# An attention and Fourier mix on one core: stack DMAs in SP's queue, and later steps for a unit's output

## The chip, the cores and the metric

The kernel runs on one core of one Trainium2 chip. The metric is the device time of one execution in microseconds (us); the kernel before has three runs, and their median is the figure. TensorE does the matrix products, VectorE (DVE), ScalarE (ACT) and GpSimd (POOL) the elementwise work, and SyncE (SP) issues most DMAs.

## What is computed

The input `A_x` has 2048 rows of 640. The output mixes two branches with a gate per row; the inputs are in float32. Cut to what matters:

```python
x = A_x
g = sigmoid((x * gate_w).sum(-1, keepdims=True))
q, k, v = split_heads(x @ wqkv)                # 32 heads of 20
p = softmax(q @ k.T * 20 ** -0.5)              # 2048 x 2048 for each head
a = merge_heads(p @ v) @ wo
re, im = x @ hid_re.T, x @ hid_im.T            # DFT along the 640
b = seq_re @ re - seq_im @ im                  # DFT along the 2048, real part
return g * a + (1 - g) * b
```

## The kernel before

**Stages.** A head stage makes queries and keys (`qk_tile`), values (`v_pair`) and the first ten tiles of the hidden DFT, and stores them in scratch memory (`qk_scr`, `v_scr`, `a_scr`). Then comes one long loop over the attention, in which the rest of the Fourier branch is done as filling work, and at last a tail: the product with `wo` and the gate. Values that need more than one pass are split in two float32r parts (`split`).

**Units and steps.** The attention is done in 32 units. A unit `n` is a pair of heads (`p = n // 2`) with one half of the queries (1024). It has 32 steps: 16 blocks of 128 keys by two chunks of 512 queries. A step multiplies scores of both heads (line 685, two matmuls), and ScalarE exponentiates them from PSUM (line 687). The row maxima that the exponential needs are found 41 steps (`LEAD`) ahead of it: the scores are made a first time the other way round (line 159), and VectorE reduces them (line 161). When all maxima of a unit are there, `max_chain` transposes them, splits them in `m1` and `m2`, and two steps later four small DMAs write them as extra rows into the query stack (lines 201 and 202). The scores of line 685 read these rows, so that the maximum is subtracted inside the product.

**Cycles.** Four steps make a cycle, in the order that the string `ORDER` gives: `e` is a score for the exponential, `m` one for the maximum, `F` a place for filling matmuls (hidden DFT, line 301, in the first 54 cycles; from cycle 57 the sequence DFT, line 523), and `B` a burst: the product of `p` and `v` for two key blocks (`av_step`, line 448), reading out finished DFT tiles, and the maxima's chain. Five PSUM banks go round among all scores.

**Places of everything else.** `at_step(i, fn)` puts `fn` into the program where step `i` begins. It sets no time: each engine works through its own instructions in the order written, and waits only for what an instruction needs. An engine can so be ahead of the steps or behind them, and what stands behind a waiting instruction on SP or GpSimd waits too.

**The stacks.** The two heads of a pair lie in one tile of keys (`kst`) and one of queries (`qst`), 128 partitions by 2048, with two buffers of each. `load_stack(p)` yields the twelve DMAs that fill them for pair `p`: four for the keys (two of 320 KB, two planes of 20 rows to 40 partitions, and two of 160 KB, 20 rows), four for the first half of the queries, and four for the second half (160 and 80 KB each). `begin` spreads them over the steps of the pair before, every other step from 2 to 24, on GpSimd's queue (line 643). The maxima of the new pair begin at step 64 - 41 = 23 of that pair; by then the first eight must be there.

**The end of a unit.** `unit_end` (line 453) copies the sums out of PSUM into `o` (line 455) and puts seven operations at steps after it: store the row sums (`store_l`), load them back spread over 128 partitions (`load_l`), their reciprocal on VectorE (`recip`), store that (`store_r`), load it back repeated (`load_r`, four DMAs), multiply on GpSimd (`norm`), store the result (`store_o`, four DMAs). All DMAs are on SP's queue, for the last unit on GpSimd's. `o`, `lc` and `rb` have one buffer each.

**The sequence DFT.** It is done in 56 blocks (`UNITS`) of 16 filling steps (`dft_step`); a block lasts about 14 steps of the attention. At `s == 0` it loads the output tiles that it will be added to (`yt`, line 511, four buffers); every eight filling steps it loads the DFT's coefficients (`load_c`, line 413), which GpSimd adds up and splits half a block later (lines 419, 102, 103). The block's result `m` is read out of PSUM in a burst; `finish_y` adds it on GpSimd (line 554) five steps later and puts the store of the tile four steps behind that (line 558). `load_a` (line 428) brings the hidden DFT's results for the next product. The raw tiles of these loads (`raw`, three buffers) are shared with the read-out of the hidden DFT (line 309).

Of the kernel before, what the change touches and what calls it, by code (L numbers as in the profile page):

```python
# [10 lines left out]
F32 = mybir.dt.float32  # L11
R = mybir.dt.float32r
# [6 lines left out]
P = 128  # L19
# [7 lines left out]
HE = D // 2  # L27
VW = 2 * (DH + 1)
KROWS = 3 * DH
NU = 2 * NP  # L30
# [25 lines left out]
UNITS = len(PRODUCTS) * HT  # L56


def f32(ap):
    return ap.bitcast(F32)  # L60
# [3 lines left out]
def mix_kernel(ctx: ExitStack, tc: tile.TileContext, xa, wqk, wb, cdft, wo, out):  # L64
    nc = tc.nc
    pe, act, dve, pool, sp = nc.tensor, nc.scalar, nc.vector, nc.gpsimd, nc.sync
    ctx.enter_context(tc.manual_schedule())

    def pools(**kw):
        return ctx.enter_context(tc.tile_pool(**kw))  # L70

    const = pools(name="const", bufs=1)
    small = pools(name="small", bufs=1)
# [9 lines left out]
    y_scr = dram.tile([NS, P, D], F32, name="y_scr")  # L83
# [28 lines left out]
    def bank():  # L112
        return ps_w.tile([P, 512], F32, name=f"ps{next(turn) % 5}")
# [13 lines left out]
    def load_stack(p):  # L127
        kt, qt = kst[p % 2], qst[p % 2]
        u = S // 2
        for t, o, two, one, cs in ((kt, D, 0, 2, slice(0, S)), (qt, 0, 1, 0, slice(0, u)), (qt, 0, 1, 0, slice(u, S))):  # L130
            for h in range(2):
                r = (2 * p + h) * DH
                b = 64 * h
                rows = slice(o + r, o + r + DH)
                yield f32(t[b + two * DH : b + (two + 2) * DH, cs]), qk_scr[:, rows, cs]
                yield f32(t[b + one * DH : b + (one + 1) * DH, cs]), qk_scr[0, rows, cs]

    def q_unit(n):
        u = n % 2 * (S // 2)
        return qst[n // 2 % 2][:, u : u + S // 2]  # L140

    mx, nms, ends = {}, {}, []
    now, later = [-1], {}

    def at_step(i, fn):
        later.setdefault(i, []).append(fn)
# [43 lines left out]
    def max_chain(n):  # L190
        q = q_unit(n)
        pt = bank()[:16, :P]
        pe.transpose(pt, nms.pop(n), ident)
        m1 = small.tile([16, P], R, name="m1", bufs=2)
        m2 = small.tile([16, P], R, name="m2", bufs=2)
        split(m1, m2, pt, dve, dve)

        def rows():
            for h in range(2):
                b = 64 * h + KROWS  # L200
                sp.dma_start(f32(q[b : b + 1, :]), f32(m1[8 * h : 8 * h + 8, :]))
                sp.dma_start(f32(q[b + 1 : b + 2, :]), f32(m2[8 * h : 8 * h + 8, :]))

        if now[0] < 0:
            rows()
        else:
            at_step(now[0] + 2, rows)


    pa = pools(name="att", bufs=1)  # L210
# [193 lines left out]
    cfin, rest = [], []  # L404

    def load_c(g):
        n, j = divmod(g, 2)
        n, t = divmod(n, HT)
        raws = []
        for i, (_, th, ri) in enumerate(PRODUCTS[n][0]):  # L410
            raw = apool[0].tile([P, 1024], F32, name="raw2", bufs=2) if i and apool else raw_tile()
            o = (2 * ri + j) * 1024
            sp.dma_start(raw, cdft[th * HT + t, :, o : o + 1024])
            raws.append(raw)

        def finish():
            c = cparts[g] = part_tile()
            if len(raws) > 1:
                pool.tensor_tensor(raws[0], raws[0], raws[1], op=ALU.add if PRODUCTS[n][0][1][0] > 0 else ALU.subtract)  # L419
            split(c[:, 0], c[:, 1], raws[0], pool, pool)  # L420

        return finish
# [28 lines left out]
            unit_end(i, n)  # L451

    def unit_end(i, n):
        o = pa.tile([P, 512], F32, name="o")
        act.activation(o, av, AF.Copy)
        lc = pa.tile([P, 16], F32, name="lc")
        rb = pa.tile([P, 512], F32, name="rb")

        q = pool if n == NU - 1 else sp

        def store_l():
            q.dma_start(l_scr[n], o.rearrange("(j r) c -> j r c", j=4)[:, DH])

        def load_l():
            q.dma_start(lc, l_scr[n].rearrange("j (a b) -> (j a) b", b=16))

        def recip():
            dve.reciprocal(lc, lc)

        def store_r():  # L470
            q.dma_start(r_scr[n].rearrange("j (a b) -> (j a) b", b=16), lc)

        def load_r():
            for j in range(4):
                q.dma_start(rb[32 * j : 32 * j + 32, :], r_scr[n, j : j + 1].to_broadcast([32, 512]))

        def norm():
            pool.tensor_tensor(o, o, rb, op=ALU.mult)  # L478

        def store_o():  # L480
            for qc in range(2):
                for h in range(2):
                    j = 2 * qc + h
                    t0 = (n % 2) * (S // 2) + qc * 512
                    r = (2 * (n // 2) + h) * DH
                    q.dma_start(o_scr[r : r + DH, t0 : t0 + 512], o[32 * j : 32 * j + DH, :])

        steps = (1, 4, 10, 12, 15, 23, 25) if n < NU - 2 else (1, 4, 10, 12, 15, 19, 21)
        for k, fn in zip(steps, (store_l, load_l, recip, store_r, load_r, norm, store_o)):
            if n == NU - 1:  # L490
                rest.append(fn)
            else:
                at_step(i + k, fn)
# [7 lines left out]
    def dft_step(g):  # L501
        n, t, s = g // NS // HT, g // NS % HT, g % NS
        if s == 0:
            new_y(0), new_y(1)
            outs[n, t] = []
            for _, th, hf in PRODUCTS[n][2]:
                tt = th * HT + t
                y = None
                if (tt, hf) in signs:
                    y = apool[0].tile([P, HE], F32, name="yt", bufs=4)  # L510
                    sp.dma_start(y, y_scr[tt, :, hf * HE : (hf + 1) * HE])
                outs[n, t].append(y)
        if s % 8 == 0 and g // 8 + 3 < 2 * UNITS:
            cfin.append(load_c(g // 8 + 3))
        if s % 8 == 4 and cfin and g // 8 + 2 < 2 * UNITS:
            cfin.pop(0)()
        c = cparts[g // 8]
        cs = slice((s % 8) * P, (s % 8 + 1) * P)
        a = at[n % 2, s]
        for z, (cz, az) in enumerate(((0, 0), (0, 1), (1, 0))):  # L520
            for h in range(2):
                r = slice(64 * h, 64 * h + 64)
                pe.matmul(yp[h][:, :HE], c[r, cz, cs], a[r, az], start=s == 0 and z == 0, stop=s == NS - 1 and z == 2)  # L523
            if z < 2:
                yield
        w = g % (HT * NS) - 16
        if n + 1 == len(PRODUCTS) and w >= 0:
            d, r = divmod(w, 8)
            if r == 0 and d < ND:
                wos[d] = raw_tile()[:, :D]  # L530
                sp.dma_start(wos[d], wo[:, d])
            if r == 5 and d < ND:
                raw = wos.pop(d)
                for h in range(2):
                    wos[d, h] = a_tile(1, 2 * d + h)
                    split(wos[d, h][:, 0], wos[d, h][:, 1], raw[:, h * HE : (h + 1) * HE], pool, pool)
        if s == NS - 1:
            m = apool[0].tile([P, HE], F32, name="m", bufs=2)
            y0, y1 = yp[0][:, :HE], yp[1][:, :HE]

            def read():
                act.activation(m, y0, AF.Copy)
                dve.tensor_tensor(m, y1, m, op=ALU.add)  # L543

            extras.append((now[0], read))
            for out_, y in zip(PRODUCTS[n][2], outs.pop((n, t))):
                extras.append((now[0] + 5, functools.partial(finish_y, out_, t, m, y)))
        yield

    def finish_y(target, t, m, y):  # L550
        sg, th, hf = target
        tt = th * HT + t
        if (tt, hf) in signs:
            pool.tensor_tensor(y, y, m, op=ALU.add if sg == signs[tt, hf] else ALU.subtract)  # L554
        else:
            signs[tt, hf] = sg
            y = m
        at_step(now[0] + 4, functools.partial(sp.dma_start, y_scr[tt, :, hf * HE : (hf + 1) * HE], y))

    preps = []  # L560

# [69 lines left out]
    def begin(i):  # L631
        now[0] = i
        n, s = divmod(i, 32)
        for fn in later.pop(i, ()):
            fn()
        if s % 2 == 0:
            flush()
        if s == 0 and n % 2 == 0:
            p = n // 2
            if p + 1 < NP:  # L640
                at_step(i + 6, functools.partial(load_v, p + 1))
                for j, args in enumerate(load_stack(p + 1)):
                    at_step(i + 2 + 2 * j, functools.partial(pool.dma_start, *args))
        if i < total:
            pts[n, s // 2, s % 2] = pair_tile()

# [90 lines left out]
    for tt in range(NS):  # L737
        y, o = ys.pop(tt), ops.pop(tt)
# [53 lines left out]
```

## Time and profile before

| what | value |
|---|---|
| median of three runs | 1954.19 us (1954.18 to 1955.42) |
| the profiled execution's own time | 1953.52 us |
| its span, first to last instruction | 1951.7 us |
| TensorE's granted clock, mean | 0.997 of full speed |
| HBM read and written | 213.81 and 63.70 MB |
| SP waiting in line 635 for `DVE raw L310` (pacing by the read-out) | 236.3 us, 52 times |
| SP waiting in line 471 for the reciprocal (pacing) | 149.5 us, 28 times |
| SP waiting in line 475 for the stored reciprocals to land | 52.0 us, 18 times |
| GpSimd waiting in line 478 for `rb` | 73.7 us, 6 times |

The span is what the profile covers; the run's own time has some 1.8 us around it. A row of the timeline is: start in us, length, engine, line of the kernel, operation, output<-inputs, shapes, count, and in brackets the idle time before it and what ended that. A row of the waits is: engine and line, what it waited for, us in total, times, the longest. A row of the windows is: from:to, length, then busy time and count for PE, PEld (weight loads), DVE, ACT and POOL, then the granted clock, the busy share of the 16 DMA engines and GB/s. A wait of SP or of GpSimd is no loss by itself: most of these waits only keep them from running further ahead.

### The profile page before, as it was taken

How to read it: one execution, taken by the hardware profiler on the slowest of the kernel's cores; microseconds unless marked ns; L12 is line 12 of the kernel's file. 1: busy time of each engine (PE TensorE's matmuls, PEld its weight loads, DVE VectorE, ACT ScalarE, POOL GpSimd, SP SyncE). 2: the span in 40 equal slices, each digit the busy share in tenths (PEclk: the TensorE clock that was granted, in tenths of full speed). 3: DMA queues.
4: the chain of work that ended last, by engine and by line, in shares of the span. 5: the costliest groups of instructions: out<-in, count | busy, mean ns of one | idle time of the engine just before them, and what ended most of it. 6: DMA issues, size and time to landing. Idle time of an engine off the chain costs nothing. (4 is left out here: it accounts for less than half of the span.)

```text
span 1951.7 us, 43695 instructions
## 1 busy us (share of the span) xinstructions
PE 1918.5 (98%) x17080; PEld 1375.4 (70%) x17080; DVE 1454.1 (75%) x2419; ACT 1211.8 (62%) x2337; POOL 1045.8 (54%) x975
## 2 busy tenths in 40 slices
PE   8999999999999999999999999999999999999999
PEld 7987767777775667666666666666666666666679
DVE  4144568889887888888888878888888887888323
ACT  4221147777776676666776766676766776776741
POOL 1210001111005989457469968995786789787512
PEclk9999999999999999999999999999999999999999
DMA  7763321212114584435356746664554565454355
GB/s 224 173 172 127 130 100 46 78 61 74 47 58 141 170 228 152 122 116 149 97 173 199 196 154 189 212 177 123 149 171 125 183 169 181 154 149 147 98 165 179
DMA packets 196414, 281.02 MB, mean 144 GB/s; under 512 B 73272, under 2 KB 137816, under 8 KB 194288
## 3 DMA queue, kind: packets, MB, share of 16 engines
q1 hardware_dynamic: 158992, 246.20, 40.8%
q0 software_dynamic: 37216, 32.03, 6.7%
q8 instruction: 134, 2.20, 0.5%
q14 instruction: 72, 0.59, 0.1%
HBM read 213.81 MB, written 63.70 MB: 142 GB/s over the span
## 5 line engine op out<-in xcount | busy, mean ns | idle before, releaser
L161 DVE TENSOR_REDUCE mx<-ps 128x1 f32<-128x512 f32 x2048 | 1287.4, 683 | 197.4 <-PE ps L159 178.8
L687 ACT ACTIVATE p<-ps 128x512 f32<-128x512 f32 x2048 | 1080.9, 598 | 443.4 <-PE ps L159 241.2
L159 PE MATMUL ps<-kst,qst 60*128 60x512 f32 x2048 | 776.1, 427 | 8.0 <-DVE mx L161 3.2
L685 PE MATMUL ps<-qst,kst 62*128 62x512 f32 x2048 | 700.7, 422 | 5.8 <-DMA qst<-m 4.2
L523 PE MATMUL yp<-a,part 64*128 64x320 f32 x5376 | 687.6, 309 | 0.1
L523 PEld LDWEIGHTS yp<-a,part 64*128 64x128 f32 x5376 | 593.7, 186 | 15.3 <-DVE m L543 0.3
L448 PE MATMUL av<-p,v 128*21 128x512 f32 x4096 | 494.4, 599 | 0.1
L685 PEld LDWEIGHTS ps<-qst,kst 62*128 62x128 f32 x2048 | 335.5, 185 | 215.2 <-DVE mx L161 181.9
L159 PEld LDWEIGHTS ps<-kst,qst 60*128 60x128 f32 x2048 | 364.5, 185 | 38.2 <-DVE mx L161 11.8
L103 POOL TENSOR_TENSOR part<-raw,part 128x1024 fp32r<-128x1024 f32 x112 | 267.2, 2386 | 9.0
L448 PEld LDWEIGHTS av<-p,v 128*21 128x21 f32 x4096 | 98.3, 100 | 226.8 <-issue 223.1
L301 PE MATMUL yp<-wb,xs 64*128 64x320 f32 x1920 | 237.4, 309 | 3.7 <-ACT raw L309 3.5
L301 PEld LDWEIGHTS yp<-wb,xs 64*128 64x128 f32 x1920 | 206.8, 187 | 8.9 <-ACT raw L309 4.1
L419 POOL TENSOR_TENSOR raw<-raw,raw 128x1024 f32<-128x1024 f32 x78 | 187.4, 2402 | 17.3 <-DMA raw<-in_cdft 11.8
L102 POOL CAST part<-raw 128x1024 fp32r<-128x1024 f32 x112 | 116.4, 1039 | 116.8 <-PE yp L523 87.4
L102 POOL CAST wb<-raw 128x966 fp32r<-128x966 f32 (+1 forms) x4 | 3.4, 856 | 215.8 <-PE ps L159 215.8
L554 POOL TENSOR_TENSOR yt<-yt,m 128x320 f32<-128x320 f32 x64 | 55.5, 878 | 111.3 <-DVE m L543 104.2
L478 POOL TENSOR_TENSOR o<-o,rb 128x512 f32<-128x512 f32 x32 | 41.4, 1294 | 134.5 <-DMA rb<-r_scr 73.7
L103 POOL TENSOR_TENSOR a<-araw,a 128x320 fp32r<-128x320 f32 x112 | 97.8, 873 | 9.0
L103 DVE TENSOR_TENSOR p<-ps,p 128x512 fp32r<-128x512 f32 x40 | 27.5, 691 | 94.1 <-ACT p L100 91.4
L106 PE MATMUL ps<-xs,part 128*128 128x512 f32 x200 | 80.2, 401 | 7.8 <-ACT xs L100 6.1
L100 ACT ACTIVATE p<-ps 128x512 fp32r<-128x512 f32 x40 | 23.7, 597 | 101.4 <-PE ps L108 101.4
(67 smaller groups left out, 1331.8 us busy)
## 6 DMA issues: line engine op xcount, KB each, us to landing
raw<-in_cdft SPq DMA_DIRECT2D x192, 512.0 KB
araw<-a_scr SPq DMA_DIRECT2D x192, 160.0 KB
qk_scr<-p SPq DMA_DIRECT2D x40, 512.0 KB
kst<-qk_scr POOLq DMA_DIRECT2D x32, 320.0 KB, 12.3
qst<-qk_scr POOLq DMA_DIRECT2D x64, 160.0 KB, 8.2
a_scr<-raw SPq DMA_DIRECT2D x64, 160.0 KB
yt<-y_scr SPq DMA_DIRECT2D x64, 160.0 KB
y_scr<-yt SPq DMA_DIRECT2D x64, 160.0 KB
```

The source lines that it names most:

```text
L102: e1.tensor_copy(dst1, src)
L103: e2.tensor_tensor(dst2, src, f32(dst1), op=ALU.subtract)
L106: pe.matmul(ps, st1, mv1, start=first, stop=False)
L159: pe.matmul(ps, q[b : b + KROWS, qt * P : (qt + 1) * P], k[b : b + KROWS, kc * 512 : (kc + 1) * 512], start=True, stop=True)
L161: return lambda: dve.tensor_reduce(mx[n][:, h, qt, kc : kc + 1], ps, axis=AX.X, op=ALU.max)
L301: pe.matmul(yp[h][:, :HE], xs[r, xz, d, cs], w[r, wz, d, :HE], start=d == 0 and z == 0, stop=d == ND - 1 and z == 2)
L419: pool.tensor_tensor(raws[0], raws[0], raws[1], op=ALU.add if PRODUCTS[n][0][1][0] > 0 else ALU.subtract)
L448: pe.matmul(av[32 * j : 32 * j + DH + 1, :], v[:, kt, h * (DH + 1) : (h + 1) * (DH + 1)], pp[qc][:, h, :], start=kt == 0, stop=kt == NS - 1)
L523: pe.matmul(yp[h][:, :HE], c[r, cz, cs], a[r, az], start=s == 0 and z == 0, stop=s == NS - 1 and z == 2)
L554: pool.tensor_tensor(y, y, m, op=ALU.add if sg == signs[tt, hf] else ALU.subtract)
L685: pe.matmul(pt, k[b : b + KROWS + 2, kt * P : (kt + 1) * P], q[b : b + KROWS + 2, qc * 512 : (qc + 1) * 512], start=True, stop=True)
L687: act.activation(pts[n, kt, qc][:, h], pt, AF.Exp, scale=float(DH) ** -0.5)
```

## The change

The twelve stack DMAs of a pair go from GpSimd's queue to SP's, at steps 4, 6, 8, 10 to 14 (the first eight) and 34, 37, 40 and 43 (the last four). A unit's seven operations go from steps 1, 4, 10, 12, 15, 23, 25 to 6, 10, 16, 23, 27, 34, 45, except for the last two units, and `o` gets a second buffer. `m1` and `m2` get one buffer in place of two. The load of `yt` goes from the first to the ninth filling step of a block, and behind the coefficient loads of the first. The store of a finished tile goes from four to eight steps behind its update.

```diff
@@ -191,8 +191,8 @@
-        m1 = small.tile([16, P], R, name="m1", bufs=2)
-        m2 = small.tile([16, P], R, name="m2", bufs=2)
+        m1 = small.tile([16, P], R, name="m1")
+        m2 = small.tile([16, P], R, name="m2")
@@ -451,7 +451,7 @@
     def unit_end(i, n):
-        o = pa.tile([P, 512], F32, name="o")
+        o = pa.tile([P, 512], F32, name="o", bufs=2)
@@ -485,7 +485,7 @@
-        steps = (1, 4, 10, 12, 15, 23, 25) if n < NU - 2 else (1, 4, 10, 12, 15, 19, 21)
+        steps = (6, 10, 16, 23, 27, 34, 45) if n < NU - 2 else (1, 4, 10, 12, 15, 19, 21)
         for k, fn in zip(steps, (store_l, load_l, recip, store_r, load_r, norm, store_o)):
@@ -503,6 +503,11 @@
         if s == 0:
             new_y(0), new_y(1)
             outs[n, t] = []
+        if s % 8 == 0 and g // 8 + 3 < 2 * UNITS:
+            cfin.append(load_c(g // 8 + 3))
+        if s % 8 == 4 and cfin and g // 8 + 2 < 2 * UNITS:
+            cfin.pop(0)()
+        if s == 8:
             for _, th, hf in PRODUCTS[n][2]:
@@ -510,10 +515,6 @@
                     sp.dma_start(y, y_scr[tt, :, hf * HE : (hf + 1) * HE])
                 outs[n, t].append(y)
-        if s % 8 == 0 and g // 8 + 3 < 2 * UNITS:
-            cfin.append(load_c(g // 8 + 3))
-        if s % 8 == 4 and cfin and g // 8 + 2 < 2 * UNITS:
-            cfin.pop(0)()
@@ -555,7 +556,7 @@
-        at_step(now[0] + 4, functools.partial(sp.dma_start, y_scr[tt, :, hf * HE : (hf + 1) * HE], y))
+        at_step(now[0] + 8, functools.partial(sp.dma_start, y_scr[tt, :, hf * HE : (hf + 1) * HE], y))
@@ -639,8 +640,8 @@
                 at_step(i + 6, functools.partial(load_v, p + 1))
-                for j, args in enumerate(load_stack(p + 1)):
-                    at_step(i + 2 + 2 * j, functools.partial(pool.dma_start, *args))
+                for j, args in zip((4, 6, 8, 10, 11, 12, 13, 14, 34, 37, 40, 43), load_stack(p + 1)):
+                    at_step(i + j, functools.partial(sp.dma_start, *args))
```

## The prediction

> **What bounds the kernel now.** I read the page first: span, busy shares, DMA queues.
>
> ```profile
> span 1951.7 us, 43695 instructions
> ## 1 busy us (share of the span) xinstructions
> PE 1918.5 (98%) x17080; PEld 1375.4 (70%) x17080; DVE 1454.1 (75%) x2419; ACT 1211.8 (62%) x2337; POOL 1045.8 (54%) x975
> ...
> q1 hardware_dynamic: 158992, 246.20, 40.8%
> ```
>
> TensorE is marked busy in 98% of the span, so at most 33 us lie open as idle, and the change adds and removes no matmul, reduce or exponential. What it can win or lose is waits of TensorE. The view of its waits says on whom:
>
> ```profile
> PE ps L685 <- DMA qst<-m: 4.2, 2, 3.3
> PE yp L301 <- ACT raw L309: 3.5, 2, 2.7
> PE ps L159 <- DVE mx L161: 3.2, 4, 1.2
> PE ps L106 <- ACT v L280: 3.0, 2, 2.6
> PE ps L159 <- DMA qst<-qk_scr: 2.4, 1, 2.4
> ```
>
> Line 685 waited for the rows of maxima, line 159 for a query stack: both are transfers that this change moves. The lines 106 are the head of the kernel, which it doesn't touch. A wait costs more than its idle time, so I measure by units: from one copy of `av` (line 455) to the next is one unit of 32 steps. The timeline of ScalarE:
>
> ```profile
> 526.02 0.60 ACT L455 ACTIVATE o<-av 128x512 f32<-128x512 f32 x1 [0.58 <-issue]
> 576.25 0.60 ACT L455 ACTIVATE o<-av 128x512 f32<-128x512 f32 x1 [0.59 <-issue]
> 631.47 0.60 ACT L455 ACTIVATE o<-av 128x512 f32<-128x512 f32 x1 [0.95 <-POOL a L102]
> ...
> 1033.45 0.60 ACT L455 ACTIVATE o<-av 128x512 f32<-128x512 f32 x1 [0.51 <-issue]
> 1083.21 0.60 ACT L455 ACTIVATE o<-av 128x512 f32<-128x512 f32 x1 [0.91 <-POOL raw L419]
> 1137.88 0.60 ACT L455 ACTIVATE o<-av 128x512 f32<-128x512 f32 x1 [2.07 <-POOL part L102]
> ...
> 1585.82 0.60 ACT L455 ACTIVATE o<-av 128x512 f32<-128x512 f32 x1 [0.91 <-issue]
> 1640.62 0.60 ACT L455 ACTIVATE o<-av 128x512 f32<-128x512 f32 x1 [0.81 <-POOL part L103]
> ```
>
> A clean unit takes 576.25 - 526.02 = 50.23 us with hidden-DFT fills and 1083.21 - 1033.45 = 49.76 us with sequence-DFT fills, 1.555 us a step. Three units are long: 55.22, 54.67 and 54.80 us, so 4.99, 4.91 and 5.04 too much. All three begin where a pair begins, that is, where a stack is loaded. In the second the wait was 3.3 us; the rest is the clock, in the table of windows:
>
> ```profile
> 1133.60:1137.00 3.40, 3.07 (x14) 0.93 (x18) 0.00 (x0) 1.09 (x2) 3.34 (x3) 0.50 0.13 45
> ```
>
> After the wait TensorE got a clock of 0.50 for 3.4 us and lost 1.7 us: 3.3 + 1.7 = 5.0, the 4.91. A wait for a DMA here costs its length plus up to 1.7 us.
>
> **Part 1: output steps and y stores.** Why were the rows late at 1134? GpSimd's and SP's timelines:
>
> ```profile
> 1123.34 1.30 POOL L478 TENSOR_TENSOR o<-o,rb 128x512 f32<-128x512 f32 x1
> ...
> 1124.67 1.42 SPq L486 DMA_DIRECT2D o_scr<-o  x4
> ...
> 1127.83 0.68 SPq L201 DMA_DIRECT2D qst<-m  x1
> ```
>
> The normalisation stands at step +23 of its unit, the store of `o` at +25, the rows at +26. GpSimd reached the normalisation 1123.34 - 1083.21 = 40.1 us after the copy; SP stood at the store until then, and the rows left at +44.6 us. Over the run SP stood there often:
>
> ```profile
> SPq L486 <- POOL o L478: 108.0, 25, 14.9
> ```
>
> After the change the normalisation stands at +34 and the store at +45, thirteen steps into the next unit. Ahead of the rows stands the store of reciprocals (+23), whose input is made at +16, seven steps (10.9 us) earlier; the load of `rb` (+27) comes behind them. The y stores go from +4 to +8, so they too leave 6.2 us more for a late GpSimd. I take the 4.91 us as gone. The four row DMAs then go out near step 26, six steps or 9.3 us before the unit that reads them, and the next thing late would be a row DMA slower than that. What the later store needs: `o` must live past +32, hence its second buffer; without it ScalarE's copy would wait 45 - 32 = 13 steps, 20 us a unit. `m1` and `m2` with one buffer are rewritten a unit (50 us) after the row DMAs that read them. Both cost nothing. The y load moves to the middle of a block, about 7 + 5 = 12 steps (18.7 us) ahead of its reader on GpSimd, with GpSimd 54% busy as cover: nothing.
>
> The reciprocal moves from +10 to +16 on VectorE:
>
> ```profile
> L468 DVE RECIPROCAL lc<-lc 128x16 f32<-128x16 f32 x32 | 7.8, 243 | 10.3 <-DMA lc<-l_scr 10.3
> ```
>
> ```profile
> 897.94 0.25 DVE L468 RECIPROCAL lc<-lc 128x16 f32<-128x16 f32 x1 [1.33 <-DMA lc<-l_scr]
> ```
>
> Same work, 0.243 us; thirty of them at a busier or an idler place of the four-step cycle are worth at most 30 x 0.243 = 7.3 us either way. I take 0. At 897.94 its load was late and VectorE stood 1.33 us, with TensorE behind it. VectorE now gets there six steps (9.3 us) later, while the load may go out as soon as the store before it has landed, at worst at its place four steps (6.2 us) later than needed now: at least 9.3 - 6.2 - 1.33 = 1.8 us to spare. So 1.33 us go.
>
> **Part 2: the stacks in SP's queue.** They cost GpSimd this:
>
> ```profile
> L635 POOL DMA_DIRECT2D qst<-qk_scr x120 | 69.4, 586 | 25.7 <-DMA kst<-qk_scr 25.6
> ```
>
> 180 issues of 0.586 us are 105 us less on GpSimd, 7 us a pair. That engine is off TensorE's path at 54%, so this is worth nothing by itself; but it makes GpSimd less late, and a stack no longer waits for GpSimd's turn. Such a wait was the 2.4 us on line 159:
>
> ```profile
> 1613.42 1.15 POOL L635 DMA_DIRECT2D qst<-qk_scr  x2
> ```
>
> ```profile
> 1622.04 0.76 PE L159 MATMUL ps<-kst,qst 60*128 60x512 f32 x1 [2.40 <-DMA qst<-qk_scr]
> ```
>
> The last two of the first eight DMAs left at 1613.42, 27.6 us after the copy at 1585.82; the reader went on at 1622.0 and had wanted them 2.4 us sooner, at 1619.6, or +33.8 us. In SP's queue the eighth stands at +14, some 20 us after the copy, or sooner where SP runs ahead. On SP twelve issues cost 12 x 0.68 us (the row at 1127.83) = 8 us a pair of 100 us, without a reader behind them. I take the 5.04 us as gone.
>
> What the trace doesn't show is how fast these transfers are from SP's queue. Here they are from GpSimd's, with SP beside them:
>
> ```profile
> 573.08 2.29 POOL L635 DMA_DIRECT2D kst<-qk_scr  x4 [22.00 <-PE ps L159]
> ...
> 576.87 0.54 SPq L462 DMA_DIRECT2D l_scr<-o  x1
> 585.24 0.31 SPq L465 DMA_DIRECT2D lc<-l_scr  x1
> ...
> 587.28 0.88 SPq L413 DMA_DIRECT2D raw<-in_cdft  x2
> ```
>
> ```profile
> 579.00:582.00 3.00, 3.00 (x34) 1.67 (x30) 2.81 (x5) 2.40 (x5) 0.00 (x0) 1.00 0.38 145
> 582.00:585.00 3.00, 3.00 (x37) 2.56 (x31) 2.51 (x5) 1.90 (x4) 0.00 (x0) 1.00 0.25 95
> ```
>
> With five stack transfers under way, 0.25 to 0.38 of 16 DMA engines were busy, 4 to 6 of them, at 95 and 145 GB/s: 23.8 GB/s each. So one stack transfer runs on one or two engines. The first eight are 1440 KB, 1.47 MB. Best: they run side by side as here, 1.47 MB / 145 GB/s = 10.2 us. Worst: all on the same two engines, 1.47 MB / 47.5 GB/s = 31.0 us. The time they have runs from 573.08, 3.2 us ahead of the copy, to +33.8: 37.0 us, of which q1's 40.8% take 15.1. That gives 11.7 us to spare or 9.1 us late. I take no wait, by the nearest row, the one with these very transfers; both ends stay in the range.
>
> [...]
>
> **Part 3: the long unit at 576.** In the last fence above `l_scr` stored at 576.87 landed only by 585.24, among the stack transfers; SP stood there, and the DFT loads behind it left at 587.28. GpSimd, then ScalarE, then TensorE (line 301, 3.5 us in two waits) followed. After the change the load of `lc` goes to +10, behind the first DFT load (+6), which can leave about 4 us sooner. The second load (+14) stays behind the stacks. I take the 4.99 us as gone; bounds 0 and 4.99.
>
> **The sum.** 4.91 + 5.04 + 1.33 + 4.99 = 16.3 us. The profiled execution took 1953.52 us (span 1951.7); 1953.52 - 16.3 = 1937.2, and the median of the runs lies 0.67 above that execution: **1938 us**.
>
> **Rivals.**
> *A, a part of it:* the waits at 1134 and 1622 go (10 us), the long unit at 576 stays, or one or two new waits of 3 to 5 us come at pair starts: 1943 to 1950. For it: at the transition the second DFT load is still behind stacks.
> *B, the change doesn't do what it says:* SP replaces GpSimd as the one that is late, because it stands at DFT loads and y stores that wait for GpSimd, and as many rows and stacks come late as now: 1950 to 1958. Against it: SP stood for `o_scr` 108 us, and those waits leave the rows' path.
> *C, slower:* the stacks share two engines and with them all of SP's traffic, so the stack is late for line 159 at pair starts. A wait like the one seen costs about 5 us (2.4 idle, the clock, and what follows: 5.04). Eleven pair starts lie in the part with dense DMA, from 640 us on. Four such waits eat most of the gain, five make it slower; eleven give 1938 + 55 = 1993, eight 1978. For it: 46.1 of 37.0 us at the worst end, and `l_scr` landing 8.4 us late in the row at 585.24. Against it: SP can issue ahead of the steps, and the eighth DMA leaves 7 us sooner than at 1613.
>
> **How the numbers follow.** Forecast (1933 to 1943; the low end has two thirds of the reciprocal's 7.3 us gained): 0.50. A: 0.20. B: 0.07. C: 0.23, since the worst end is past the 37.0 us while the nearest row is well inside. Faster by over 0.2% (below 1950.3) holds the forecast and A, 0.70; within 0.2%, about what a measurement of this kernel can tell from no change, is B, 0.07; slower is C, 0.23. The range runs from 1933 to 1965: it leaves out the larger two thirds of C.
>
> **What would show it.** In the changed profile: no DMA issues of line 635 on POOL; rows of `qst<-m` never over 40 us after the copy; units at 576, 1083 and 1586 at 50 us; no clock of 0.50 after 640 us. Wrong: TensorE waits `L159 <- DMA kst` or `qst<-qk_scr` at many pair starts (C); `DVE lc <- DMA` growing (part 1); `L301 <- ACT raw` staying (part 3); `yp L523 <- POOL part`, were DFT loads held up behind the stacks.

## The result and the profile after

The changed kernel takes 1984.07 us (five runs, 1978.51 to 1986.03), the kernel before 1955.42 us in the runs beside it: a ratio of 1.0138 (95% interval 1.0119 to 1.0158), 1.4% slower. The forecast was 1938 us, the range 1933 to 1965. The time lies outside that range, where rival C put it.

The view of TensorE's waits, after (engine and line, what it waited for, us in total, times, longest):

```profile
PE ps L159 <- DMA qst<-qk_scr: 22.3, 4, 7.6
PE yp L301 <- ACT raw L309: 7.6, 1, 7.6
PE ps L106 <- ACT xs L100: 6.7, 1, 6.7
PE ps L159 <- DMA raw<-in_cdft: 5.7, 1, 5.7
```

The rows of maxima (`qst<-m`) are gone from it. In their place the scores of line 159 wait for the query stack, 22.3 us where it was 2.4. The 5.7 us put down to `raw<-in_cdft` stand at the same line, at the start of another pair; line 159 reads only the two stacks, so these too are taken for a stack here. The wait near the end of the hidden DFT (line 301) has grown from 3.5 to 7.6 us. The copies of `av` show which units are long:

```profile
575.95 0.60 ACT L455 ACTIVATE o<-av 128x512 f32<-128x512 f32 x1 [0.58 <-issue]
636.95 0.60 ACT L455 ACTIVATE o<-av 128x512 f32<-128x512 f32 x1 [0.90 <-PE av L448]
...
1201.69 0.60 ACT L455 ACTIVATE o<-av 128x512 f32<-128x512 f32 x1 [0.91 <-issue]
1260.98 0.60 ACT L455 ACTIVATE o<-av 128x512 f32<-128x512 f32 x1 [0.54 <-PE av L448]
```

These two take 61.00 and 59.29 us where 50.2 and 49.7 are clean. Five more are long, and all seven begin with a pair: together they hold 53.7 us too much, each 2.1 to 10.8, where the three of before held 14.9. The first of them is the one with the wait of line 301; in each of the other six line 159 waited once, 1.9 to 7.6 us. The other units with a stack to load are clean, some cleaner than before.

SP's timeline at the unit that begins at 1201.69 (start, length, line, transfer):

```profile
1198.28 0.64 SPq L636 DMA_DIRECT2D kst<-qk_scr  x1
...
1202.72 0.56 SPq L462 DMA_DIRECT2D l_scr<-o  x1
1211.83 0.63 SPq L636 DMA_DIRECT2D kst<-qk_scr  x1
1212.51 0.89 SPq L428 DMA_DIRECT2D araw<-a_scr  x2
1213.89 0.29 SPq L636 DMA_DIRECT2D kst<-qk_scr  x1
1217.09 0.34 SPq L465 DMA_DIRECT2D lc<-l_scr  x1
...
1235.65 1.07 SPq L636 DMA_DIRECT2D qst<-qk_scr  x2
```

and TensorE's, and two windows (from:to, length, busy time of PE, PEld, DVE, ACT, POOL, granted clock, busy share of 16 DMA engines, GB/s):

```profile
1243.54 0.76 PE L159 MATMUL ps<-kst,qst 60*128 60x512 f32 x1 [7.56 <-DMA qst<-qk_scr]
```

```profile
1210.00:1213.00 3.00, 3.00 (x36) 2.11 (x36) 2.94 (x6) 2.30 (x6) 1.07 (x2) 1.00 0.13 48
```

```profile
1240.30:1247.00 6.70, 3.46 (x18) 2.32 (x22) 2.61 (x5) 0.74 (x2) 6.41 (x6) 0.50 0.89 272
```

Four things are to be seen. From 1210 to 1213, 0.13 x 16 = 2 DMA engines were busy, at 48 GB/s together, and 14 had nothing to do; SP stood until 1211.83. SP stood 9.1 us between the store of the row sums and the next stack DMA, and the load of those sums left 14.4 us after their store. The last two of the first eight stack DMAs left at 1235.65, 34.0 us after the copy, where the prediction had some 20. And line 159 waited 7.56 us, until 1243.54; the clock fell to 0.50 while it waited, and of the 6.7 us at that clock TensorE worked in 3.46.

The issue of the eighth stack DMA separates the pairs. In the six where line 159 waited it left 28.0 to 34.6 us after the copy; in the eight others that begin with a copy, 21.4 to 26.3 us.

SP's own waits name the stacks:

```profile
SPq L636 <- DMA kst<-qk_scr: 64.9, 17, 8.6
...
SPq L465 <- DMA l_scr<-o: 50.2, 20, 9.7
```

Why SP waits for a stack that it doesn't need shows when its DMAs are counted in the trace. Together its lines waited for the landing of a stack 78 times, 244 us, and each of these waits ended with the landing of the transfer eight places ahead in SP's order. Of all its 172 waits for a landing (362 us) 144 (298 us) did so; most of the others are the load of the row sums waiting for their store.

The timeline above has one of them: eight places ahead of the stack DMA at 1211.83 stands the one at 1198.28, 320 KB of keys. SP waited until that one had landed, 13.5 us after its issue.

GpSimd did get lighter, as foreseen (1045.8 us before, 975 instructions):

```profile
PE 1925.0 (97%) x17080; PEld 1380.5 (70%) x17080; DVE 1458.0 (73%) x2419; ACT 1212.0 (61%) x2337; POOL 943.9 (48%) x795
```

### The profile page after: what moved, and what is told of

Its sections match the earlier page's. It is cut to its first block, busy times and chain, and to the rows that moved or that the text cites. A ratio compares the mean times of both kernels' runs of the same rounds, so it can differ in the third digit from the quotient of the medians.

```text
span 1984.3 us, 43667 instructions
## 1 busy us (share of the span) xinstructions
PE 1925.0 (97%) x17080; PEld 1380.5 (70%) x17080; DVE 1458.0 (73%) x2419; ACT 1212.0 (61%) x2337; POOL 943.9 (48%) x795
## 5 line engine op out<-in xcount | busy, mean ns | idle before, releaser
L159 PE MATMUL ps<-kst,qst 60*128 60x512 f32 x2048 | 779.7, 428 | 34.0 <-DMA qst<-qk_scr 22.3
L301 PEld LDWEIGHTS yp<-wb,xs 64*128 64x128 f32 x1920 | 208.8, 190 | 12.3 <-ACT raw L309 7.9
L419 POOL TENSOR_TENSOR raw<-raw,raw 128x1024 f32<-128x1024 f32 x78 | 186.9, 2396 | 48.2 <-DMA raw<-in_cdft 34.6
L433 POOL TENSOR_TENSOR araw<-araw 128x320 f32<-128x320 f32 x80 | 69.9, 874 | 33.3 <-DMA araw<-a_scr 27.0
```

Source lines behind the costliest of these rows:

```text
L159: pe.matmul(ps, q[b : b + KROWS, qt * P : (qt + 1) * P], k[b : b + KROWS, kc * 512 : (kc + 1) * 512], start=True, stop=True)
L301: pe.matmul(yp[h][:, :HE], xs[r, xz, d, cs], w[r, wz, d, :HE], start=d == 0 and z == 0, stop=d == ND - 1 and z == 2)
```

## The experiments

**Theory T:** the stack DMAs of two planes onto 40 partitions run on two DMA engines (0.13 of 16 from 1210 to 1213), side by side from SP's queue on the same two, and make what SP has beside them late (the load of the row sums left 14.4 us after their store). **Q:** it is the stacks' place in SP's queue, not their width. **U:** it is the later unit steps and y moves. The first four ran side by side; the kernel before took 1957.16 us there.

### The same DMAs, spread wider (wide12)

The rows of a stack are put in another order, so that the outer dimension on both sides is 20 or 40 rows, not 2 planes. Twelve DMAs, the same bytes, the same steps; the three products of the parts stay the same.

```diff
-                yield f32(t[b + two * DH : b + (two + 2) * DH, cs]), qk_scr[:, rows, cs]
-                yield f32(t[b + one * DH : b + (one + 1) * DH, cs]), qk_scr[0, rows, cs]
+                pair = qk_scr[:, rows, cs].rearrange("z r c -> r z c")
+                if t is qt:
+                    pair = qk_scr[0, rows, cs].unsqueeze(1).to_broadcast([DH, 2, cs.stop - cs.start])
+                yield f32(t[b : b + 2 * DH, cs]), pair
+                yield f32(t[b + 2 * DH : b + 3 * DH, cs]), qk_scr[int(t is qt), rows, cs]
```

> The changed kernel with the rows of a stack in another order (two planes of a row side by side, 20 by 2 on both sides), twelve DMAs from SP's queue of the same bytes at the same steps. [...] Rival Q (it is the place in SP's queue: stacks leave late behind SP's other waits, whatever their width): 1975 to 1990 us, the waits stay. Rival U (the later unit steps and y moves cost it): 1975 to 1990 us.

Measured: 1932.56 us (ratio to before 0.9874, 0.9857 to 0.9891), 51 us under the changed kernel. TensorE's waits begin so (line 162 is the 159 of before):

```profile
PE ps L106 <- ACT xs L100: 6.3, 1, 6.3
PE ps L162 <- DVE mx L164: 1.7, 2, 0.8
PE ps L106 <- ACT part L100: 1.3, 1, 1.3
```

No wait for a stack or for rows is left, and no unit in the loop is over 51.0 us; Q and U had 1975 us or more. Two windows show the width. In each a 320 KB key transfer is under way in a quiet part, first in the changed kernel, then here:

```profile
378.50:380.50 2.00, 2.00 (x22) 1.01 (x23) 2.00 (x4) 1.41 (x4) 0.00 (x0) 1.00 0.16 57
```

```profile
376.30:377.30 1.00, 1.00 (x16) 1.00 (x14) 0.95 (x2) 1.00 (x3) 0.00 (x0) 1.00 0.58 205
```

The busy share was 0.16, some 2.6 engines, and is 0.58, some 9. SP hardly stands for stacks any more: over all its lines 12 us, where the changed kernel has 244. At the unit that begins at 1173.58 the last two of the first eight left 18.4 us after the copy:

```profile
1191.95 1.56 SPq L639 DMA_DIRECT2D qst<-qk_scr  x2
```

Over all pairs the eighth left 9.7 to 20.6 us after the copy, at the steps of the changed kernel. T holds; Q and U fall, since places and steps are those of the changed kernel.

### The parts one by one (steps_only, stack_only, pool_new)

steps_only is the changed kernel with the old loop on GpSimd:

```diff
-                for j, args in zip((4, 6, 8, 10, 11, 12, 13, 14, 34, 37, 40, 43), load_stack(p + 1)):
-                    at_step(i + j, functools.partial(sp.dma_start, *args))
+                for j, args in enumerate(load_stack(p + 1)):
+                    at_step(i + 2 + 2 * j, functools.partial(pool.dma_start, *args))
```

> The changed kernel with the stack DMAs back on GpSimd's queue at steps 2 to 24, all else of the change kept. T and Q: the three long units of before shorten since the rows no longer stand behind the store of o, 1938 to 1950 us. U: 1975 us or more.

Measured: 1939.62 us (0.9914, 0.9897 to 0.9931). One long unit is left, 54.25 us, the one that began at 1586 in the kernel before. As there, line 159 waits for the query stack:

```profile
PE ps L159 <- DMA qst<-qk_scr: 3.0, 1, 3.0
```

stack_only is the kernel before with those same two lines the other way round.

> The kernel before with the stack DMAs alone moved to SP's queue at the new steps; unit steps, buffers and y moves as before. T and Q: as slow as the changed kernel or slower, 1975 to 2000 us, because the load of lc (step 4) and the reciprocal (step 10) are now close behind the stacks. U: 1955 us or less.

Measured: 2017.42 us (1.0311, 1.0294 to 1.0328), 17 us above the expected range. So the move to SP costs 60 us alone, and the rest of the change wins back 33 of them. The waits show the same reader:

```profile
PE ps L159 <- DMA qst<-qk_scr: 29.5, 7, 6.4
PE ps L159 <- DVE mx L161: 7.4, 5, 2.3
PE ps L159 <- DMA rb<-r_scr: 6.6, 1, 6.6
```

pool_new keeps the new steps for the stacks, but on GpSimd:

```diff
-                    at_step(i + j, functools.partial(sp.dma_start, *args))
+                    at_step(i + j, functools.partial(pool.dma_start, *args))
```

> The changed kernel with the stack DMAs on GpSimd's queue, but at the new steps 4 to 14 and 34 to 43; width as before. T: the narrow DMAs go over changing engines and SP's loads aren't held up, 1936 to 1950 us. Q: the same. A rival to both, that the new places of the stacks are too late for the reader: waits of line 159 as in the changed kernel, 1970 us or more.

Measured: 1941.88 us (0.9927, 0.9910 to 0.9945). The queue alone, with the same narrow DMAs at the same steps, makes 42 us between this and the changed kernel. So it isn't the width alone either: it is narrow DMAs in SP's queue. From GpSimd's queue they didn't all run on the same two engines: in the kernel before 4 to 6 were busy with five stack transfers under way, three of them two-plane (0.25 and 0.38 of 16, the prediction's windows).

### How much is narrow (planes, planesK, planesQ)

The first of these splits each two-plane DMA in two of one plane, and puts the second at the place of the first; the other two do so for the keys or the queries alone (`if p and t is kt`, `if p and t is qt`).

```diff
-                yield f32(t[b + two * DH : b + (two + 2) * DH, cs]), qk_scr[:, rows, cs]
+                if p:
+                    for z in range(2):
+                        yield f32(t[b + (two + z) * DH : b + (two + z + 1) * DH, cs]), qk_scr[z, rows, cs]
+                else:
+                    yield f32(t[b + two * DH : b + (two + 2) * DH, cs]), qk_scr[:, rows, cs]
```

> The changed kernel with each two-plane stack DMA split into two DMAs of one plane (20 rows to 20 partitions), eighteen DMAs for a pair in place of twelve, at the same places. Theory T (bytes on two engines): one-plane DMAs are spread wider, so like wide12, 1930 to 1940 us. Rival N (it is the number of stack transfers in SP's queue that holds it up, since each transfer waits for the landing of the one eight ahead): no better than the changed kernel, 1975 us or more; half-way, 1950 to 1975, if both.

> Only the key stack split into planes; the queries stay two-plane: 320 KB of the first eight left on two engines, 6.9 us of them. T: late at few pair starts or none, 1930 to 1945 us, less than planesQ. N: fourteen transfers a pair, four of them slow; slower than planesQ or the same.

> Only the query stacks split into planes; the keys stay two-plane: 640 KB left on two engines, 13.8 us of them. T: between planesK and the changed kernel, 1940 to 1970 us. N: two slow transfers a pair are left, faster than planesK.

The 6.9 and 13.8 us of two engines, and the 20.7 us expected of the burst below, are estimates: 320, 640 and 960 KB at the 47.5 GB/s that the prediction worked out for two engines. That one-plane DMAs run wider shows in the changed kernel: from 1734.0 to 1734.5 the busy share was 0.12, 2 engines; from 1734.6 to 1736.0, with a one-plane transfer of 160 KB (issued at 1734.03) beside the two-plane ones, it was 0.54, 8.6 engines.

Measured beside a kernel before of 1955.54 us (the changed kernel beside one of 1955.42):

| kernel | narrow bytes among the first eight | us | ratio (95%) |
|---|---|---|---|
| planes | 0 KB | 1936.51 | 0.9911 (0.9884 to 0.9938) |
| planesK | 320 KB | 1938.26 | 0.9918 (0.9894 to 0.9942) |
| planesQ | 640 KB | 1945.08 | 0.9948 (0.9931 to 0.9965) |
| changed kernel | 960 KB | 1984.07 | 1.0138 (1.0119 to 1.0158) |

Eighteen quick transfers do nearly as well as the twelve of wide12 (0.9911 and 0.9874), so N falls. The time rises with the narrow bytes, little up to 640 KB and steeply above: TensorE in planesQ waits for a stack once (line 163 is the 159 of before), in the changed kernel four times for 22.3 us:

```profile
PE ps L163 <- DMA qst<-qk_scr: 1.6, 1, 1.6
```

### All eight at once (burst)

```diff
-                for j, args in zip((4, 6, 8, 10, 11, 12, 13, 14, 34, 37, 40, 43), load_stack(p + 1)):
+                for j, args in zip((4, 4, 4, 4, 4, 4, 4, 4, 34, 37, 40, 43), load_stack(p + 1)):
```

> The changed kernel, stacks two-plane as in it, but the first eight DMAs of a pair all at step 4 of SP's queue. It asks what makes the stack late in the changed kernel. Theory L (SP issues the last ones late, because each transfer waits for the landing of the one eight ahead and for others' waits between them): together they leave at once, 20.7 us of two engines end some 20 to 25 us after the copy, and line 159 waits for no stack; what lands behind them may be late instead (lc, DFT loads), 1940 to 1970 us. Theory E (the two engines have too little time for stacks and everything else in the 37 us, in whatever order): lateness only changes hands, 1975 to 1995 us.

Measured: 2028.93 us (1.0365, 1.0347 to 1.0384), outside both guesses on the slow side. L was right that line 159 then waits for no stack, and E that the lateness changes hands: it is now VectorE that waits for `lc`, and TensorE at line 686 for VectorE:

```profile
DVE lc L468 <- DMA lc<-l_scr: 75.6, 14, 8.6
```

```profile
PE ps L686 <- DVE mx L161: 29.0, 9, 5.5
```

The burst also shows the engines best. In a quiet part SP issued all eight between 379 and 387 us:

```profile
379.06 2.37 SPq L636 DMA_DIRECT2D kst<-qk_scr  x4
381.53 5.81 SPq L636 DMA_DIRECT2D qst<-qk_scr  x4
388.96 0.35 SPq L636 DMA_DIRECT2D a_scr<-raw  x1
390.13 0.34 SPq L440 DMA_DIRECT2D v<-v_scr  x1
396.47 0.57 SPq L462 DMA_DIRECT2D l_scr<-o  x1
397.69 0.31 SPq L636 DMA_DIRECT2D a_scr<-raw  x1
406.28 0.32 SPq L465 DMA_DIRECT2D lc<-l_scr  x1
```

```profile
384.00:387.00 3.00, 3.00 (x34) 2.20 (x28) 2.39 (x5) 1.90 (x5) 0.00 (x0) 1.00 0.12 48
393.00:396.00 3.00, 3.00 (x35) 2.38 (x36) 2.93 (x5) 2.41 (x6) 0.00 (x0) 1.00 0.14 57
399.50:401.50 2.00, 2.00 (x24) 1.82 (x21) 1.95 (x4) 1.59 (x4) 0.00 (x0) 1.00 0.13 51
```

Four two-plane transfers had been issued by 384, and in each of the three windows 0.12 to 0.14 of 16 engines worked, two, at 48 to 57 GB/s. (Between the windows the share is higher at times, with a store and the load of `v` under way.) At that rate, by estimate, their 960 KB take 17 to 21 us. So the four ran on the same two engines; on engines of their own they would have kept more than two busy. From GpSimd's queue the same transfers side by side had kept 4 to 6 busy. The 8 KB store of the row sums, issued at 396.47, ahead of the last of these windows, took 9.8 us to land, and only then, at 406.28, could the load of `lc` leave. Here SP stood for that store and not for a stack: so a transfer behind the narrow ones can also be late by its own landing.

### The steps without narrow stacks (wide_old_steps, before_wide)

wide_old_steps is stack_only with the rows of wide12; before_wide is the kernel before, stacks on GpSimd, with the rows of wide12 and nothing else.

> The kernel before with the stacks on SP at the new steps and with rows in the order of wide12, so that each DMA is spread wide; unit steps, buffers and y moves as before. T: most of the 60 us that stack_only lost against before comes back, 1935 to 1955 us; what is left above wide12 is the worth of the later unit steps when the stacks are quick. A rival, that the unit steps were needed for any stack on SP: 1975 us or more.

Measured: 1934.28 us (0.9896, 0.9874 to 0.9917). This is just below the range. With quick stacks the later unit steps, the second `o` and the y moves are worth nothing that can be told from wide12.

> The kernel before with the stacks still on GpSimd's queue and only the order of their rows changed as in wide12. If the three long units of before come from a late GpSimd (the prediction's reading), two of them stay: 1945 to 1955 us. If they come from slow narrow transfers on that queue as well, they go: 1936 to 1944 us.

Measured: 1937.67 us (0.9902, 0.9884 to 0.9919). Two of the three long units of before go with the order of rows alone (49.96 us both, where they were 55.22 and 54.80). The one of 1083 still takes 51.97 us, and the rows of maxima are still waited for (line 688 is the 685 of before):

```profile
PE ps L688 <- DMA qst<-m: 2.0, 1, 2.0
```

The DMA issues of before_wide, with the time to landing in the last column (12.3 and 8.2 us in the kernel before):

```profile
kst<-qk_scr POOLq DMA_DIRECT2D x32, 320.0 KB, 5.9
qst<-qk_scr POOLq DMA_DIRECT2D x64, 160.0 KB, 5.5
```

## Why the prediction was wrong

**What failed: "I take no wait, by the nearest row".** The bounds were 11.7 us to spare and 9.1 us late. The row taken for the value showed these transfers from GpSimd's queue, on 4 to 6 engines at 95 and 145 GB/s, and that number belonged to the queue. From SP's it is two engines at some 50 GB/s, and the changed kernel came in by the other end: at 1243.54 the stack was 7.56 us late. That this lies inside the bound is luck in part, since the bound let SP issue in time. Nor did "both ends stay in the range" hold: 9.1 us at each of rival C's eleven pair starts are 100 us, and the range ends 27 above the forecast. In the burst four such DMAs, of keys and of queries, kept two engines busy (0.12 to 0.14 of 16).

**The time in the sum was that of an SP that doesn't stand.** "The eighth stands at +14, some 20 us after the copy, or sooner" was measured as 34.0 us. With quick transfers it holds (9.7 to 20.6 us in wide12). With slow ones SP stands until the transfer eight places ahead has landed (64.9 us for `kst` in line 636) and issues the last of the stack late. The burst shows that the issue isn't the root: issued at once, the stack is in time, and `lc` is late instead. The root is narrow transfers on two engines out of sixteen.

**Part 1 was right for the rows.** steps_only has no wait for the rows of maxima, and the unit of 1083 takes 49.95 us there. The chain told in Part 1 (a late GpSimd, the store of `o`, the rows) is borne out by before_wide too: with quick stacks GpSimd still reaches the normalisation of that unit 39.5 us after the copy (40.1 before), and the rows are still waited for. Of the whole sum, 16.3 us, 11.2 are left without the stack move's 5.04; steps_only gained 15.8 between the profiled executions (1953.52 and 1937.77).

**Part 2's gain (5.04 us) came only with quick transfers.** The unit that is long at 1586 takes 49.62 us in wide12 and 57.00 in the changed kernel. It is clean in before_wide as well (49.96), where GpSimd still issues the eighth stack DMA 24.7 us after the copy (28.2 before): the wait there was put down to GpSimd's turn, but in part it was the transfer's length.

**Part 3 failed with its sign.** The unit at 576 grew from 55.22 to 61.00 us (in steps_only it is clean, 49.92 us). The first DFT load did leave sooner (584.40 in place of 587.28), but the second left later (602.65 in place of 599.61), behind the stacks. What TensorE waited for in the end wasn't that load, as Part 3 had it: ScalarE stood for a store of an earlier tile, the last of which SP had issued at 599.85, and TensorE for ScalarE, 7.6 us in one piece:

```profile
608.65 0.44 ACT L309 ACTIVATE raw<-yp 128x320 f32<-128x320 f32 x1 [8.32 <-DMA a_scr<-raw]
```

**VectorE's reciprocal:** "at least 1.8 us to spare" failed. Three waits for `lc`, 2.83, 1.12 and 0.82 us, are in the changed kernel where two (1.33 and 0.32) were before. In steps_only and wide12, with the same unit steps, there is none, so the steps were right and the narrow stacks took the margin. (A wait of 8.6 us in the last units is in all of these kernels.)

**Rival C** had the mechanism and its place; that its 1978 us came so near is partly luck, since two terms were off in opposite ways. It counted eight late pair starts at about 5 us. There were seven long units, six at line 159 and one at line 301, at 7.7 us each on the average. The seven waits are 37.5 us. TensorE further worked 28.4 us at a clock of 0.50 around them, which costs half of that, 14.2: together 51.7 of the 53.7 us. Compared with the same units before, the seven are 38.3 us longer and all others 5.5 shorter. That is 32.9, and the profiled executions differ by 32.5 (1953.52 and 1986.03). C had 0.23; the trace of before had no row of SP's queue for a two-plane transfer, and a price from another queue's rows was taken for one.

What stays open: how the harm divides between the two engines' own time and SP's standing for the transfer eight ahead. Both are seen, and no run took away the one and left the other.

## What to carry to other kernels

Before moving a transfer to another queue, ask on how many DMA engines it runs there. The table of windows tells: busy share x 16 in a stretch where it is alone. A transfer that turns out narrow, as those with an outer dimension of 2 did here (2 engines, some 9 with the rows in the other order), is worth another order of rows: here that gave 51 us without another instruction. Here a few slow transfers made what was issued behind them late (8 KB of row sums took 9.8 us to land in the burst), and held up the queue itself (SP stood 244 us for stacks). A price is taken from rows of the same queue, or the bound is kept as likely.

## What the runs showed beside it

What a wait costs beside its length can't be read from its length. In the kernel before, a wait of 3.3 us was followed by one stretch of 3.4 us at a clock of 0.50, and the prediction took 1.7 us from it as the most. After the change most such stretches were 6.8 us long, and how much of them fell into the wait itself differed. Around the wait of 7.56 us TensorE worked 3.5 us at half clock, which costs 1.75 us. Around a wait of 3.55 us (it ended at 1449.39) it worked 5.86 us at half clock, which costs 2.9:

```profile
1240.21:1247.04 6.83, 3.50 (x21) 2.33 (x25) 2.61 (x5) 0.78 (x2) 6.54 (x6) 0.50 0.88 268
1448.42:1455.25 6.83, 5.86 (x30) 2.68 (x30) 2.61 (x5) 1.08 (x2) 4.48 (x8) 0.50 0.78 245
```

The best version here is wide12, at 1932.56 us 1.3% under the kernel before.
